# Sigmoid attention and a GELU feed-forward block on one core: a float64 weight decoder that reads raw words two bytes further on

## The chip, the cores and the metric

The program runs on one core of a Trainium2 chip. The metric is the time of one execution in microseconds on the device, as the median of several runs. The engines of the core run side by side, each through its own list of instructions in order: TensorE (PE in the profile; its weight loads are a row of their own, PEld), VectorE (DVE), ScalarE (ACT), GpSimd (POOL, which here only issues transfers) and SyncE (SP, which issues most of the loads). They wait for one another through semaphores.

## The reference

Attention without a softmax, with a sigmoid in its place, and then a two-layer feed-forward block over its output:

```python
batch, n_heads, seq, head_dim = (8, 12, 448, 64)
scores = scale * np.matmul(q, k.transpose(0, 1, 3, 2)) - np.log(S)
attn = 1.0 / (1.0 + np.exp(-scores))
attn_out = np.matmul(attn, v)                      # then [3584 tokens, 768]
h = x @ w_in                                       # 768 x 2048
g = 0.5 * h * (1.0 + erf(h * inv_sqrt2))
return g @ w_out                                   # 2048 x 768
```

`q`, `k` and `v` are fp32. `w_in` and `w_out` come out of the setup as float64, since an fp32 array is multiplied with a float64 scalar. The host only lays the data out anew, so the kernel gets the weights as 64-bit words and makes fp32 of them itself.

## The kernel before

**Attention** is a loop over 24 units of four heads (`u`, 0 to 23; batch `u // 3`). A unit's scores are six tiles of 128 keys by 2 x 448 queries, in the order (p, c) = (0,0), (0,1), (0,2), (1,0), (1,1), (1,2); each is made by six matmuls on q and k split in two fp32r parts (L381). ScalarE turns each tile into a sigmoid (L359). Then `values(u)` multiplies the sigmoids with v (L414) in two passes; between the passes come a tiny VectorE copy called `mark` (L441), for which TensorE waits, and the last 64 keys of the next unit (L398). At the end of a unit, `park` copies the result out of PSUM with two VectorE copies (L453) and sends it to DRAM.

PSUM has four slots of two banks for all this. `place` alternates them, so that the result of unit u (`pav`) lies in the slot that the fourth score tile, (1,0), of unit u + 1 takes. That tile's first weight load therefore waits for both L453 copies.

**The feed-forward block** starts directly after the last unit (L526 for all matmuls). Each weight tile of 128 x 768 is loaded from scratch DRAM (`wst`), copied to fp32r on ScalarE (L255, the high part) and subtracted on VectorE (L262, the low part). The first weight pass (`ffn1_plain`) takes 16 such tiles: steps (0,0), (1,0), (2,0), (3,0) for the first token half, then (0,1), (1,1), (2,1), (3,1), then (4,0) and so on; a step has 18 matmuls. `whl` has four buffers, so tile 4 is prepared only once (0,1) is through. The second token half, `x1`, is loaded when attention ends and split by two casts on ScalarE (L290) and two subtractions on VectorE (L291). Later blocks use sums and differences of quarter weights (a seven-product scheme); for `w_out` these come from `mix`, four VectorE instructions of 512 columns on four decoded quarters, whose results go to DRAM through POOL. `mix` has one output tile `s`, so a second `mix` waits until the transfers of the first are through.

**The weight decoder** runs beside attention and the first weight pass. It is a generator (`Decoder.work`); `dec.go(n)` emits the next n steps where it is called. In a unit that is `decode(u, 0)`, after the scores, and `decode(u, 1)`, inside `meanwhile`, behind `mark`. For a chunk i, `start(i)` makes mantissa and exponent (three VectorE instructions), `scale(i)` runs two ScalarE passes, `end(i)` puts the result together (two VectorE instructions) and issues the raw load of chunk i + 3. `STEPS` says how many steps a unit takes at each place, (1, 2) unless listed; in the feed-forward block `dec.to` spreads the rest over the weight tiles. There are 16 chunks of `w_in` (768 columns) and 24 of `w_out` (512 columns).

The order of all this is written out by hand: the pools run under a manual schedule, and the queues keep the program order.

Of the kernel before, what the change touches and what calls it, by code (L numbers as in the profile page):

```python
# [8 lines left out]
F32 = mybir.dt.float32  # L9
F32R = mybir.dt.float32r  # L10
U32 = mybir.dt.uint32
I32 = mybir.dt.int32
I64 = mybir.dt.int64
# [3 lines left out]
P = 128  # L17
# [4 lines left out]
def tile_sigmoid_attention_gelu_ffn(  # L22
# [27 lines left out]
    def psum(name, bufs):  # L50
# [11 lines left out]
    RAW = 2 * max(WU, 2 * S)  # L62
# [39 lines left out]
    class Decoder:  # L102
# [7 lines left out]
        def load(self, i):  # L110
            if i < len(CHUNKS):
                kind, u, c0, w = CHUNKS[i][:4]
                src = (w_in if kind == "in" else w_out)[u].rearrange("p a b -> p (a b)")
                raw = sb.tile([P, RAW], U32, tag="raw", name=f"raw{i}", bufs=3)[:, : 2 * w]
                nc.sync.dma_start(raw.bitcast(I64), src[:, c0 : c0 + w])
                self.raws[i] = raw.rearrange("p (n t) -> p n t", t=2)

        def start(self, i):
            w = CHUNKS[i][3]
            low, high = self.raws[i][:, :, 0], self.raws[i][:, :, 1]  # L120
            me = sb.tile([P, 2 * WU], U32, tag="me", name=f"me{i}", bufs=2)
            m, e = me[:, :w], me[:, WU : WU + w]
# [7 lines left out]
            self.parts[i] = m, e  # L130

        def scale(self, i):
            e = self.parts[i][1]
# [5 lines left out]
        def end(self, i):  # L139
            kind, u, c0, w, ij, group = CHUNKS[i]  # L140
            high = self.raws.pop(i)[:, :, 1]
            m, e = self.parts.pop(i)
# [768 lines left out]
```

## Time and profile before

| | |
|---|---|
| median of 3 runs | 1024.38 us (1023.8 to 1024.64) |
| the profiled execution | 1023.69 us, span 1021.9 us |
| TensorE busy | 1017.6 us |
| VectorE busy | 726.0 us |
| ScalarE busy | 652.5 us |
| POOL busy | 116.4 us |
| attention, from its first score tile to the feed-forward block's first matmul | 4.27 to 241.79 us |
| TensorE's clock granted | 0.999 of full speed |

The span runs from the first to the last instruction; the time of the execution has 1.8 us more around it. The profile's own times are counted from the start of the span. The profiled execution lies 0.69 us under the median of the runs.

### The profile page before, as it was taken

To read this page: it belongs to the slowest core of one execution; us is meant where nothing else is said; L and a number is where in the kernel's file an instruction comes from. 1 tells how busy PE (TensorE), PEld (TensorE's weight loads), DVE (VectorE), ACT (ScalarE), POOL (GpSimd) and SP (SyncE) were. 2 spreads that over 40 slices of the span, in tenths; PEclk is the share of its full clock that TensorE was granted. 3 is DMA by queue.
4 is the path that set the end of the run, shared out by engine and by line. 5 is a ranking of instruction groups with operands and counts; after the bars stand their busy time and mean duration, and the time that the engine had idled before them with its cause. 6 is when DMAs were issued, how large, how long until landed. Compare 5 with 4: busy or idle time off the path is not lost.

```text
span 1021.9 us, 16631 instructions
## 1 busy us (share of the span) xinstructions
PE 1017.6 (100%) x6478; PEld 921.9 (90%) x6478; DVE 726.0 (71%) x903; ACT 652.5 (64%) x912; POOL 116.4 (11%) x186
## 2 busy tenths in 40 slices
PE   9999999999999999999999999999999999999998
PEld 5656656667999999999999999999999999999998
DVE  3777777885899698795378887434888764368873
ACT  5888887785455466557666655666656467666652
POOL 0111112101332362224000001000000000000000
PEclk9999999999999999999999999999999999999999
DMA  9999899996788797689444445634444553334441
GB/s 265 298 321 322 307 325 303 341 288 226 241 273 278 255 326 274 212 305 337 123 131 126 141 133 166 212 123 126 132 113 147 154 161 113 120 100 133 138 136 67
DMA packets 85998, 211.86 MB, mean 207 GB/s; under 512 B 9440, under 2 KB 35936, under 8 KB 85920
## 3 DMA queue, kind: packets, MB, share of 16 engines
q1 hardware_dynamic: 69136, 153.82, 49.8%
q0 software_dynamic: 14880, 55.26, 15.1%
q10 hardware_dynamic: 1904, 1.72, 0.5%
q8 instruction: 51, 0.84, 0.3%
q14 instruction: 27, 0.22, 0.1%
HBM read 163.38 MB, written 50.33 MB: 209 GB/s over the span
## 4 chain that ended last, share of the span: by engine, by line
PE 99%; DMA 0%; ACT 0%; SPq 0%; issue 0%; ACTq 0%
PE pf L526 76%; PE pav L414 12%; PE sc L381 9%; PE sc_t L398 2%; PE pav L429 0%; PE warm L468 0%; DMA out_dram<-tmp 0%; ACT tmp L784 0%; ACT tmp L779 0%; SPq L728 0%; ACTq L779 0%
## 5 line engine op out<-in xcount | busy, mean ns | idle before, releaser
L526 PE MATMUL pf<-op,whl 128*128 128x448 f32 x2016 | 382.0, 353 | 0.0
L526 PEld LDWEIGHTS pf<-op,whl 128*128 128x128 f32 x2016 | 381.1, 189 | 0.3
L255 ACT CAST whl<-wst 128x768 fp32r<-128x768 f32 x212 | 176.3, 833 | 202.0 <-PE pf L526 185.1
L262 DVE TENSOR_TENSOR whl<-wst,whl 128x768 fp32r<-128x768 f32 x212 | 202.1, 954 | 138.8 <-ACT whl L255 138.5
L526 PE MATMUL pf<-xh_p,whl 128*128 128x448 f32 x1008 | 273.5, 353 | 0.0
L526 PEld LDWEIGHTS pf<-xh_p,whl 128*128 128x128 f32 x1008 | 190.7, 189 | 0.1
L526 PE MATMUL pf<-xl_p,whl 128*128 128x448 f32 x504 | 177.7, 353 | 0.0
L359 ACT ACTIVATE a<-sc 128x896 f32<-128x896 f32 x144 | 119.3, 935 | 32.2 <-PE sc L381 32.2
L414 PE MATMUL pav<-a,v 64*64 64x448 f32 x1296 | 132.8, 541 | 0.0
L563 DVE TENSOR_TENSOR op<-g,op 128x896 fp32r<-128x896 f32 x112 | 121.3, 1083 | 6.6 <-ACT op L573 6.6
L414 PEld LDWEIGHTS pav<-a,v 64*64 64x64 f32 x1296 | 55.1, 132 | 61.3 <-issue 34.6
L573 ACT CAST op<-g 128x896 fp32r<-128x896 f32 x112 | 104.7, 936 | 2.6 <-PE pf L526 2.6
L526 PE MATMUL pf<-xh,whl 128*128 128x448 f32 x384 | 104.3, 353 | 0.0
L526 PEld LDWEIGHTS pf<-xl_p,whl 128*128 128x128 f32 x504 | 95.4, 189 | 0.0
L526 PEld LDWEIGHTS pf<-xh,whl 128*128 128x128 f32 x384 | 72.6, 189 | 0.7 <-issue 0.7
L563 DVE TENSOR_TENSOR g<-g,g 128x896 f32<-128x896 f32 x64 | 69.3, 1083 | 0.0
L526 PE MATMUL pf<-xl,whl 128*128 128x448 f32 x192 | 67.7, 353 | 0.0
L560 ACT ACTIVATE g<-pf 128x448 f32<-128x448 f32 x80 | 41.9, 537 | 20.1 <-PE pf L526 20.1
L134 ACT ACTIVATE me<-me 128x512 f32<-128x512 int32 (+1 forms) x40 | 29.6, 741 | 33.8 <-DVE me L123 33.8
L381 PE MATMUL sc<-lo,hi 64*128 64x448 f32 x276 | 51.2, 367 | 0.0
L351 DVE TENSOR_TENSOR lo<-qk,hi 128x896 fp32r<-128x896 f32 x46 | 50.1, 1089 | 1.1
L381 PE MATMUL sc<-hi,lo 64*128 64x448 f32 x276 | 48.8, 349 | 0.0
(82 smaller groups left out, 875.6 us busy)
## 6 DMA issues: line engine op xcount, KB each, us to landing
wst<-scr_out SPq DMA_DIRECT2D x112, 384.0 KB, 3.1
wst<-scr_in SPq DMA_DIRECT2D x84, 384.0 KB, 3.1
v<-v_dram SPq DMA_DIRECT2D x24, 512.0 KB, 8.0
raw<-w_in_dram SPq DMA_DIRECT2D x16, 768.0 KB, 5.0
raw<-w_out_dram SPq DMA_DIRECT2D x24, 512.0 KB, 5.3
scr_x<-x POOLq DMA_DIRECT2D x24, 448.0 KB, 7.8
qk<-q_dram SPq DMA_DIRECT2D x23, 448.0 KB, 10.1
qk<-k_dram SPq DMA_DIRECT2D x46, 224.0 KB, 10.4
```

What stands on the lines that cost most here:

```text
L134: nc.scalar.activation(e.bitcast(F32), e.bitcast(I32), AF.Relu, bias=1151.0 * 2**23, scale=-8.0)
L255: nc.scalar.copy(hl[:, 0], t)
L262: nc.vector.tensor_tensor(hl[:, 1], t, hl[:, 0], op=ALU.subtract)
L351: nc.vector.tensor_tensor(lo, raw, hi, op=ALU.subtract)
L359: nc.scalar.activation(to, sc, AF.Sigmoid, bias=NEG_LOG_S, scale=SCALE)
L381: nc.tensor.matmul(sc[:, j], ks[rows(j), 1, keys], braid(qs[rows(j), 0]) if braided else qs[rows(j), 0], start=n == 0, stop=n == last,)
L398: nc.tensor.matmul(sc[rows(p), j], raw[rows(j), p, 1, FULL * P :], raw[rows(j), p, 0], start=True, stop=True,)
L414: nc.tensor.matmul(pav[rows(j), p], vals[u][half, p, j, c], a[p][half, j], start=not swap and c == order[0], stop=c == (order[-1], FULL - ...
L526: nc.tensor.matmul(bank, a, braid(m), **flags)
L560: nc.scalar.activation(straight(dst), unbraid(src), AF.Gelu)
L563: nc.vector.tensor_tensor(out, a, b, op=op)
L573: nc.scalar.copy(op[:, 0], src)
```

## The change

Each raw load starts two bytes later in the row. Of every 64-bit word, the first 32-bit word in SBUF then holds bits 16 to 47, and the third 16-bit half holds the top 16 bits (sign, exponent, four bits of mantissa). ScalarE reads that half as a 16-bit integer, strided by 8 bytes, and makes of it the upper part of the fp32 pattern as a 32-bit integer, in two passes. VectorE then needs three instructions for a chunk, all in `end`: shift the word right by 13 and OR it with the upper part, take the rounding bit out of the word (in place), and add the two as integers. `start` is gone, and a chunk has two steps instead of three. The chunks of `w_out` are 1024 columns wide and 12 instead of 24. `STEPS` is new: (1, 1) unless listed, and half the pace in units 18 to 21. The raw tiles grow from 1792 to 2048 words, and the pool of sigmoid tiles shrinks from 11 to 8.

```diff
-    RAW = 2 * max(WU, 2 * S)
+    RAW = 2 * max(WU, 2 * S, 2 * QUAD)
...
-    CHUNKS = [("in", u, 0, WU, 0, 0) for u in range(NF)] + [
-        ("out", 2 * ee + h, c * QUAD, QUAD, ij, (c, e))
+    CHUNKS = [(w_in[u : u + 1].rearrange("r p a b -> p r (a b)"), WU, "in", u, 0, 0) for u in range(NF)]
+    CHUNKS += [
+        (w_out_part(c, e + KE * i), 2 * QUAD, "out", 0, 2 * QUAD * i, (c, e))
         for c in range(2)
         for e in range(KE)
-        for ij, (ee, h) in enumerate(((e, 0), (e, 1), (e + KE, 0), (e + KE, 1)))
+        for i in range(2)
     ]
...
         def load(self, i):
-                raw = sb.tile([P, RAW], U32, tag="raw", name=f"raw{i}", bufs=3)[:, : 2 * w]
-                nc.sync.dma_start(raw.bitcast(I64), src[:, c0 : c0 + w])
+                src = CHUNKS[i][0].bitcast(U16)
+                dst = raw.bitcast(U16)[:, : 4 * w].rearrange("p (r n) -> p r n", r=rows)
+                nc.sync.dma_start(dst[:, :, : 4 * w // rows - 1], src[:, :, 1:])
...
-        def start(self, i):
-            nc.vector.tensor_scalar(e, high, 0x7FF00000, None, op0=ALU.bitwise_and)
-            nc.vector.tensor_scalar(
-                m, high, 11, 0x80000000, op0=ALU.logical_shift_left, op1=ALU.bitwise_or
-            )
-            nc.vector.scalar_tensor_tensor(
-                m, low, 21, m, op0=ALU.logical_shift_right, op1=ALU.bitwise_or
-            )
...
         def scale(self, i):
-            nc.scalar.activation(
-                e.bitcast(F32), e.bitcast(I32), AF.Relu, bias=1151.0 * 2**23, scale=-8.0
-            )
-            nc.scalar.activation(e, e.bitcast(F32), AF.Relu, bias=255.0 * 2**23, scale=-1.0)
+            half = self.raws[i].bitcast(I16)[:, : 4 * w].rearrange("p (n t) -> p n t", t=4)
+            nc.scalar.activation(
+                top.bitcast(F32), half[:, :, 2], AF.Prelu, bias=-LEAST, scale=-1.0, alpha=TINY
+            )
+            nc.scalar.activation(
+                top.bitcast(I32),
+                top.bitcast(F32),
+                AF.Prelu,
+                bias=-LEAST * 2.0**20,
+                scale=-(2.0**19) / TINY,
+                alpha=TINY,
+            )
...
         def end(self, i):
-            nc.vector.scalar_tensor_tensor(
-                e, high, 0x80000000, e, op0=ALU.bitwise_and, op1=ALU.bitwise_or
-            )
-            nc.vector.scalar_tensor_tensor(
-                self.out[:, ij * QUAD : ij * QUAD + w],
-                m,
-                2.0**-31,
-                e.bitcast(F32),
-                op0=ALU.mult,
-                op1=ALU.mult,
-            )
+            nc.vector.scalar_tensor_tensor(
+                bits, words, 13, top, op0=ALU.logical_shift_right, op1=ALU.bitwise_or
+            )
             nc.vector.tensor_scalar(
+                words, words, 12, 1, op0=ALU.logical_shift_right, op1=ALU.bitwise_and
             )
+            nc.vector.tensor_tensor(bits, bits, words, op=ALU.add)
...
-            self.start(0)
-            yield
             for i in range(len(CHUNKS)):
                 self.scale(i)
-                yield
-                if i + 1 < len(CHUNKS):
-                    self.start(i + 1)
                 yield
                 self.end(i)
                 self.load(i + 3)
...
-    STEPS = {2: (1, 1), B * NU - 1: (4, 4)}
+    STEPS = {18: (1, 0), 19: (0, 1), 20: (1, 0), 21: (0, 1)}
...
-            a = at.tile([P, 2, S], F32, tag="a", name=f"a{u}_{p}_{c}", bufs=11)
+            a = at.tile([P, 2, S], F32, tag="a", name=f"a{u}_{p}_{c}", bufs=8)
...
-                dec.go(STEPS.get(u, (1, 2))[place])
+                dec.go(STEPS.get(u, (1, 1))[place])
...
-                dec.to(done + (2 + 3 * len(CHUNKS) - done) * (f + 1) / (NF - 3))
+                dec.to(done + (1 + 2 * len(CHUNKS) - done) * (f + 1) / (NF - 3))
```

The integer add is built as an instruction that the listing calls ISA; it reads each 32-bit word as two 16-bit halves, which is why its row has twice the columns. The new file is three lines shorter ahead of the attention code, so L438 there is the `mark` copy (L441 before), L450 is `park` (L453 before) and L259 is the low part (L262 before).

The first place is VectorE in unit 19, from the copy `mark` to `park`. `raw16` and `me16` belong to chunk 16, the first of `w_out`; `xl0_0` is a part of the first token half's low part, made in this unit because it is one of the last. Before:

```order
L123 TENSOR_SCALAR me17_2491<-raw17_2270 128x512
L124 TENSOR_SCALAR me17_2491<-raw17_2270 128x512
L127 SCALAR_TENSOR_TENSOR me17_2491<-raw17_2270,me17_2491 128x512
L441 COPY ones_63<-pav19_2495 128x2
L143 SCALAR_TENSOR_TENSOR me16_2365<-raw16_2141,me16_2365 128x512
L148 SCALAR_TENSOR_TENSOR wd16_2514<-me16_2365 128x512
L495 TENSOR_TENSOR xl0_0_2171<-xl0_0_2171,xh0_0_2170 128x1344
L453 COPY x19_2541<-pav19_2495 128x448 x2
```

The same place in the changed kernel:

```order
L438 COPY ones_63<-pav19_2456 128x2
L151 SCALAR_TENSOR_TENSOR wd16_2474<-raw16_2000,me16_2339 128x1024
L154 TENSOR_SCALAR raw16_2000<-raw16_2000 128x1024
L157 ISA wd16_2474<-raw16_2000,wd16_2474 128x2048
L492 TENSOR_TENSOR xl0_0_2147<-xl0_0_2147,xh0_0_2146 128x1344
L450 COPY x19_2501<-pav19_2456 128x448 x2
```

The three instructions ahead of `mark` are gone, and between `mark` and the copies out of PSUM there are now three of 1024 columns instead of two of 512. Unit 21 reads alike, with two L259 subtractions where L492 stands here; unit 22 has the three alone.

The second place is VectorE at the start of the feed-forward block, from the first `mix` (output `s0_0`) to the low part of weight tile 4 (`whl4`). Before:

```order
L99 TENSOR_TENSOR s0_0_3108<-wd16_2514,s0_0_3108 128x512
L123 TENSOR_SCALAR me24_3184<-raw24_3007 128x512
L124 TENSOR_SCALAR me24_3184<-raw24_3007 128x512
L127 SCALAR_TENSOR_TENSOR me24_3184<-raw24_3007,me24_3184 128x512
L143 SCALAR_TENSOR_TENSOR me23_3011<-raw23_2974,me23_3011 128x512
L148 SCALAR_TENSOR_TENSOR wd20_2972<-me23_3011 128x512
L96 TENSOR_TENSOR s0_1_3190<-wd20_2972 128x512
L97 TENSOR_TENSOR s0_1_3190<-s0_1_3190,wd20_2972 128x512
L98 TENSOR_TENSOR s0_1_3190<-wd20_2972 128x512
L99 TENSOR_TENSOR s0_1_3190<-wd20_2972,s0_1_3190 128x512
L262 TENSOR_TENSOR whl4_3180<-wst4_2766,whl4_3180 128x768
```

The same place in the changed kernel:

```order
L107 TENSOR_TENSOR s0_0_3034<-wd16_2474,s0_0_3034 128x512
L104 TENSOR_TENSOR s0_1_3046<-wd18_2831 128x512
L105 TENSOR_TENSOR s0_1_3046<-s0_1_3046,wd18_2831 128x512
L106 TENSOR_TENSOR s0_1_3046<-wd18_2831 128x512
L107 TENSOR_TENSOR s0_1_3046<-wd18_2831,s0_1_3046 128x512
L151 SCALAR_TENSOR_TENSOR wd20_3123<-raw20_2711,me20_3120 128x1024
L154 TENSOR_SCALAR raw20_2711<-raw20_2711 128x1024
L157 ISA wd20_3123<-raw20_2711,wd20_3123 128x2048
L259 TENSOR_TENSOR whl4_3118<-wst4_2714,whl4_3118 128x768
```

The second `mix` follows the first at once, and a chunk's three instructions stand behind it and ahead of the low part of tile 4; before, the decoder's work stood between the two `mix` blocks and the low part came right behind the second.

## Rows read from the trace of the kernel before

**Rows 1.** The page's first part: busy us, share of the span, instructions of TensorE and others.
```profile
PE 1017.6 (100%) x6478; PEld 921.9 (90%) x6478; DVE 726.0 (71%) x903; ACT 652.5 (64%) x912; POOL 116.4 (11%) x186
```
**Rows 2.** Stretches of one unit: length, busy us of PE, PEld, DVE, ACT, POOL, clock, DMA.
```profile
16.66:26.61 9.95, 9.95 (x103) 5.93 (x102) 5.08 (x8) 6.71 (x8) 0.84 (x1) 1.00 1.06 323
36.42:46.24 9.82, 9.82 (x103) 6.12 (x102) 7.67 (x11) 8.83 (x11) 1.29 (x2) 1.00 1.07 258
...
85.48:95.29 9.81, 9.81 (x102) 6.09 (x102) 7.67 (x11) 8.27 (x10) 1.28 (x2) 1.00 0.96 309
```
**Rows 3.** The chain that ended last, by time: start us, us, what.
```profile
203.19 3.60 PE sc L381 x36
...
222.81 3.60 PE sc L381 x36
...
241.79 774.28 PE pf L526 x4092
```
**Rows 4.** Timeline of unit 8, ScalarE and VectorE: start us, us, what.
```profile
92.00 0.84 ACT L137 ACTIVATE me<-me 128x768 uint32<-128x768 f32 x1
92.34 0.16 DVE L441 COPY ones<-pav 128x2 f32<-128x2 f32 x1 [1.02 <-PE pav L414]
95.37 1.16 DVE L453 COPY x<-pav 128x448 f32<-128x448 f32 x2 [1.02 <-PE pav L414]
```
**Rows 5.** Timeline of unit 20, TensorE's weight loads: the fourth score tile, the first value.
```profile
204.74 0.19 PEld L381 LDWEIGHTS sc<-lo,hi 64*128 64x128 f32 x2
...
206.72 0.21 PEld L414 LDWEIGHTS pav<-a,v 64*64 64x64 f32 x8 [0.28 <-ACT a L359]
```
**Rows 6.** Groups by line and form: busy us, mean ns of one, idle before.
```profile
L262 DVE TENSOR_TENSOR whl<-wst,whl 128x768 fp32r<-128x768 f32 x212 | 202.1, 954 | 138.8 <-ACT whl L255 138.5
L563 DVE TENSOR_TENSOR op<-g,op 128x896 fp32r<-128x896 f32 x112 | 121.3, 1083 | 6.6 <-ACT op L573 6.6
L573 ACT CAST op<-g 128x896 fp32r<-128x896 f32 x112 | 104.7, 936 | 2.6 <-PE pf L526 2.6
L563 DVE TENSOR_TENSOR xl_p<-x,xh_p 128x1344 fp32r<-128x1344 f32 x12 | 18.7, 1556 | 7.3 <-ACT xh_p L586 7.3
L143 DVE SCALAR_TENSOR_TENSOR me<-raw,me 128x768 uint32<-128x768 uint32 x16 | 15.5, 969 | 0.0
L137 ACT ACTIVATE me<-me 128x768 uint32<-128x768 f32 x16 | 13.5, 843 | 0.5
L123 DVE TENSOR_SCALAR me<-raw 128x768 uint32<-128x768 uint32 x16 | 9.0, 563 | 0.0
```
**Rows 7.** Timeline of VectorE in unit 19.
```profile
200.24 0.16 DVE L441 COPY ones<-pav 128x2 f32<-128x2 f32 x1 [0.87 <-PE pav L414]
...
201.76 1.55 DVE L495 TENSOR_TENSOR xl<-xl,xh 128x1344 fp32r<-128x1344 f32 x1
203.28 1.15 DVE L453 COPY x<-pav 128x448 f32<-128x448 f32 x2
```
**Rows 8.** Timeline of VectorE in unit 21.
```profile
219.86 0.16 DVE L441 COPY ones<-pav 128x2 f32<-128x2 f32 x1 [0.88 <-PE pav L414]
...
223.00 1.15 DVE L453 COPY x<-pav 128x448 f32<-128x448 f32 x2
```
**Rows 9.** Timeline of VectorE at the start of the feed-forward block.
```profile
255.30 1.56 DVE L291 TENSOR_TENSOR xl<-xl,xh 128x1344 fp32r<-128x1344 f32 x1 [2.34 <-ACT xh L290]
...
264.75 0.69 DVE L96 TENSOR_TENSOR s<-wd 128x512 f32<-128x512 f32 x1 [1.79 <-DMA scr_out<-s]
...
266.69 0.68 DVE L99 TENSOR_TENSOR s<-wd,s 128x512 f32<-128x512 f32 x1
267.29 0.95 DVE L262 TENSOR_TENSOR whl<-wst,whl 128x768 fp32r<-128x768 f32 x1
```
**Rows 10.** The load of v issued in unit 3 (L334): duration ns, start us; issue to landing.
```profile
L334 SPq DMA_DIRECT2D v<-v_dram x1: 379/379/379, 44.8 to 44.8; - x1
...
DMA to landing us min/median/max: 9.3/9.3/9.3
```

More of the change, by code (lines that the diff above doesn't have):

```diff
@@ L12 @@
 I32 = mybir.dt.int32
-I64 = mybir.dt.int64
+I16 = mybir.dt.int16
+U16 = mybir.dt.uint16
 AF = mybir.ActivationFunctionType
@@ L85, in tile_sigmoid_attention_gelu_ffn, with w_out_part @@
     }
-    CHUNKS = [("in", u, 0, WU, 0, 0) for u in range(NF)] + [
-        ("out", 2 * ee + h, c * QUAD, QUAD, ij, (c, e))
+    LEAST, TINY = 896.0 * 16, 2.0**-40
+    def w_out_part(c, ee):
+        src = w_out[2 * ee : 2 * ee + 2].rearrange("h p a b -> p h (a b)")
+        return src[:, :, c * QUAD : c * QUAD + QUAD]
+    CHUNKS = [(w_in[u : u + 1].rearrange("r p a b -> p r (a b)"), WU, "in", u, 0, 0) for u in range(NF)]
+    CHUNKS += [
+        (w_out_part(c, e + KE * i), 2 * QUAD, "out", 0, 2 * QUAD * i, (c, e))
         for c in range(2)
         for e in range(KE)
-        for ij, (ee, h) in enumerate(((e, 0), (e, 1), (e + KE, 0), (e + KE, 1)))
+        for i in range(2)
     ]
@@ L111, in load @@
             if i < len(CHUNKS):
-                kind, u, c0, w = CHUNKS[i][:4]
-                src = (w_in if kind == "in" else w_out)[u].rearrange("p a b -> p (a b)")
-                raw = sb.tile([P, RAW], U32, tag="raw", name=f"raw{i}", bufs=3)[:, : 2 * w]
-                nc.sync.dma_start(raw.bitcast(I64), src[:, c0 : c0 + w])
-                self.raws[i] = raw.rearrange("p (n t) -> p n t", t=2)
-        def start(self, i):
-            w = CHUNKS[i][3]
-            low, high = self.raws[i][:, :, 0], self.raws[i][:, :, 1]
-            me = sb.tile([P, 2 * WU], U32, tag="me", name=f"me{i}", bufs=2)
-            m, e = me[:, :w], me[:, WU : WU + w]
-            nc.vector.tensor_scalar(e, high, 0x7FF00000, None, op0=ALU.bitwise_and)
+                src = CHUNKS[i][0].bitcast(U16)
@@ new lines, in load, with scale @@
+                rows, w = src.shape[1], CHUNKS[i][1]
+                raw = sb.tile([P, RAW], U32, tag="raw", name=f"raw{i}", bufs=3)
+                dst = raw.bitcast(U16)[:, : 4 * w].rearrange("p (r n) -> p r n", r=rows)
+                nc.sync.dma_start(dst[:, :, : 4 * w // rows - 1], src[:, :, 1:])
+                self.raws[i] = raw
+        def scale(self, i):
+            w = CHUNKS[i][1]
+            me = sb.tile([P, 2 * WU], U32, tag="me", name=f"me{i}", bufs=2)
+            self.parts[i] = top = me[:, :w]
+            half = self.raws[i].bitcast(I16)[:, : 4 * w].rearrange("p (n t) -> p n t", t=4)
[10 more added lines that the diff above has]
+            )
@@ new lines, in end @@
+        def end(self, i):
+            _, w, kind, u, at, group = CHUNKS[i]
+            words = self.raws.pop(i)[:, : 2 * w].rearrange("p (n t) -> p n t", t=2)[:, :, 0]
+            top = self.parts.pop(i)
+            if at == 0:
+                self.out = sb.tile([P, 4 * QUAD], F32, tag="wd", name=f"wd{i}", bufs=2)
+            bits = self.out[:, at : at + w].bitcast(U32)
+            nc.vector.scalar_tensor_tensor(
+                bits, words, 13, top, op0=ALU.logical_shift_right, op1=ALU.bitwise_or
+            )
@@ L124, in start @@
             nc.vector.tensor_scalar(
-                m, high, 11, 0x80000000, op0=ALU.logical_shift_left, op1=ALU.bitwise_or
+                words, words, 12, 1, op0=ALU.logical_shift_right, op1=ALU.bitwise_and
             )
-            nc.vector.scalar_tensor_tensor(
-                m, low, 21, m, op0=ALU.logical_shift_right, op1=ALU.bitwise_or
-            )
-            self.parts[i] = m, e
-        def scale(self, i):
-            e = self.parts[i][1]
-            nc.scalar.activation(
-                e.bitcast(F32), e.bitcast(I32), AF.Relu, bias=1151.0 * 2**23, scale=-8.0
-            )
-            nc.scalar.activation(e, e.bitcast(F32), AF.Relu, bias=255.0 * 2**23, scale=-1.0)
@@ L139, in end @@
[L139 to L142, printed above, removed]
-            nc.vector.scalar_tensor_tensor(
-                e, high, 0x80000000, e, op0=ALU.bitwise_and, op1=ALU.bitwise_or
-            )
-            if ij == 0:
-                self.out = sb.tile([P, 4 * QUAD], F32, tag="wd", name=f"wd{i}", bufs=2)
-            nc.vector.scalar_tensor_tensor(
-                self.out[:, ij * QUAD : ij * QUAD + w],
-                m,
-                2.0**-31,
-                e.bitcast(F32),
-                op0=ALU.mult,
-                op1=ALU.mult,
-            )
+            nc.vector.tensor_tensor(bits, bits, words, op=ALU.add)
@@ L158, in end @@
                 self.done += 1
-            elif ij == 3:
+            elif at + w == 4 * QUAD:
                 self.pending.append((group, self.out))
```

## The prediction

> **What bounds the kernel now.** I read the busy times first. TensorE is busy for 1017.6 of 1021.9 us [rows 1], so no other engine's saving can be worth more than about 4 us unless that row hides waits. Whether it does is told by the units of attention: unit 1, in which the decoder does nothing yet, lasts 9.95 us with 5.08 us of VectorE work; units 3 and 8 carry a chunk each, 7.67 us of VectorE work, and last 9.82 and 9.81 us [rows 2]. The decoder costs TensorE nothing today. In the feed-forward block 4092 matmuls take 774.28 us [rows 3], 0.189 us apiece without a gap. So there is nothing to win, and the question is only whether the new order makes TensorE wait.
>
> **Where TensorE could wait for VectorE in attention.** The fourth score tile of a unit takes the PSUM slot that both L453 copies of the unit before must empty. In unit 8 the copies start at 95.37 and end 1.16 us later, at 96.53 [rows 4]; the next unit starts at 95.29. In unit 20, which starts at 203.19 [rows 3], the first weight load of the fourth tile stands at 204.74 [rows 5], so it is needed 1.55 us after a unit's start, which is 96.84 for unit 9. The copies have a margin of 0.31 us. What they exceed it by stops TensorE, less some of the 0.28 us that it waits there for a sigmoid anyway [rows 5]; I credit 0.2.
>
> **Prices.** VectorE's two-source instructions take 954, 1083 and 1556 ns at 768, 896 and 1344 columns [rows 6], 1.056 ns a column. The shift with OR has L143's form: 0.97 us at 768 columns, 1.24 at 1024. The rounding bit has L123's: 0.56 us (its 563 ns for 768 columns is far under a column a cycle of the others), and at half the slope 0.70 for 1024; it writes strided, which no row does, so its upper bound is the full rate of L143, 0.97 and 1.24. The integer add has no like in the trace. It reads 1536 or 2048 halves. Its lower bound is L262's rate, a word a step: 0.95 us, and 0.95 + 256 x 1.056 = 1.22 us. Its upper bound is a half a step: 1556 + 192 x 1.056 = 1.76 us, and 1556 + 704 x 1.056 = 2.30 us. The halves of a word lie side by side, and L143 reads just such strided words at the rate of L262, so the lower end is nearer; I take a quarter of the way up, 1.15 and 1.5. With 0.05 us of gaps a chunk costs 2.73 us (768) or 3.49 us (1024) of VectorE.
>
> The Trainium skill, "VectorE: DVE Perf Modes", What auto-detection actually checks, says that an instruction whose tensors are all 16-bit with step one runs two elements a cycle. By it the add would stand at its lower end and the sum below would be about 1.1 us smaller. No row of before has a 16-bit instruction, so the trace neither bears this out nor contradicts it.
>
> **Units 2 to 17: nothing.** Before, `end` came a unit after `scale`; now it follows in the same unit, so the first VectorE instruction waits for the second ScalarE pass. That ended at 92.84 [rows 4], after `mark` at 92.34, which stays ahead. The ScalarE passes are two as before, at the same place of its queue; the first reads strided 16-bit numbers, which I price like L137, 843 ns [rows 6]. Then 92.87 + 2.73 = 95.60, and the copies can start at about 95.52 instead of 95.37: 0.15 of the margin of 0.31 is used. At the upper bounds the chain would be 1.0 us longer and each unit would lose about 0.6 us, 16 times: some 9 us. The removed instructions ahead of `mark` stood in VectorE's idle time (1.02 us before `mark` [rows 4]), so they give nothing back.
>
> SP's queue moves too: the raw load waits for its buffer until the add is through, about 2 us later, and the loads of v, q and k stand behind it. It also comes one unit earlier at the start (unit 2 instead of 3), where the DMA engines are full (1.07 [rows 2]). The tightest is v of unit 5: issued at 44.8, landed 9.3 us later, at 54.1 [rows 10]. Unit 5 starts two units after 36.42, at 56.04, and its values come 3.5 us later (206.72 against 203.19 [rows 3, 5]), at 59.6. With 2.4 us of later issue and a raw load more in front (0.79 MB at some 300 GB/s [rows 2], 2.6 us) it lands at 59.1. I put nothing in the sum, and up to 2 us in the range. The eight sigmoid buffers cost nothing: seven are used in a unit, and TensorE ends a unit's values before it begins the next scores.
>
> **Unit 19: 1.4 us.** VectorE goes from `mark` at 200.24 to the copies at 203.28 with two 512-column instructions and the 1.55 us of L495 [rows 7]. Now: 200.32 + 3.49 = 203.81, L495 until 205.28, the copies from 205.2 to 206.36 (successive instructions overlap by 0.08). They are needed at 203.19 + 1.55 = 204.74. Late by 1.62; less 0.2 is 1.4 us.
>
> **Unit 21: 1.65 us.** `mark` at 219.86 [rows 8]; 219.94 + 3.49 = 223.43; two low parts, 1.82 us, until 225.17; the copies until 226.25, needed at 222.81 + 1.55 = 224.36. Late by 1.89, less 0.2.
>
> **Unit 22: 0.5 us.** Scale and end fall together with 1024 columns. In unit 8 the second pass ended 7.36 us after the unit's start; at ScalarE's slope ((936 - 843) / 128 = 0.73 ns a column [rows 6]) each pass is 0.19 us longer, so it ends at 7.74, and VectorE at 7.74 + 3.49 = 11.23, the copies at 12.3. Needed: 9.81 + 1.55 = 11.36. That is 0.95 late, less 0.2, less what unit 22 has already been held up in its middle by unit 21's copies, which stops TensorE more than ScalarE. I take 0.5, between 0 and 0.8. Units 18 and 20 only scale, and a pass longer by 0.19 us meets the wait for the next unit's scores.
>
> **Start of the feed-forward block: 2.6 us.** Step (4,0) comes after 8 steps of 18 matmuls, 144 x 0.189 = 27.25 us after 241.79 [rows 3]: at 269.04 it needs the low part of tile 4, which was ready at 267.29 + 0.95 = 268.24 [rows 9], a margin of 0.8 us. The second `mix` can't start before the transfers of the first have left `s` (264.75, released by DMA), and ends at 267.37 [rows 9]. Before, the decoder's work stood in that wait; now both `mix` blocks follow one another, the wait is empty, and a chunk of 3.49 us stands between the second `mix` and the low part: 267.29 + 3.49 = 270.78, the low part from 270.7 to 271.65. Late by 2.6 us. Afterwards VectorE catches up: a chunk less than every 6.8 us, so later tiles are ready in time. The split of `x1` is close too: its last low part ends at 256.86 [rows 9] and is needed half a step into (0,1), at 241.79 + 13.6 + 1.7 = 257.1. The raw load of 1 MB that now falls beside its transfers may cost up to 1 us; I put 0 in the sum.
>
> **The sum.** 1.4 + 1.65 + 0.5 + 2.6 = 6.15 us on the profiled execution's 1023.69, of which the span is 1021.9: 1029.8 us. The median of the runs lies 0.69 above it, so 1030.5 us. With the add at its lower end the four terms are 5.1 us together. With add and rounding bit at their upper ends each of the four chains is 1.3 us longer, and the ordinary units lose as well: 6.15 + 5.2 + 9 = 20 us, 1044.7.
>
> **The rivals.** *Hidden after all: 1024.4 to 1026.4 us.* A margin that I don't see takes the delays, such as first `mix` transfers that land earlier because no raw load runs beside them, by 2.6 us; then 268.1 is reached and two or three us are left of the sum, or less. Against it: the rows give the two late copies without a transfer in them. *Faster: about 1018 us.* If TensorE's busy row hid waits for ScalarE, 0.28 us in each of 23 units is 6 us, and less VectorE work could free some of it. It decides only if a unit without decoding is shorter, and unit 1 is not [rows 2]. *The ordinary units stall as well: 1034 to 1045 us*, if the add takes a half a step or the strided write halves the rounding bit's rate; the margin of 0.31 us decides, and 0.2 us more per unit is 3 us. *The shifted load is slow: 1045 us and more.* Raw loads are 0.79 of some 3 MB a unit (9.81 us at 309 GB/s); if each took twice the DMA time, a unit's share would go from 0.96 to 1.2 [rows 2] and 16 units would grow by about 2 us each, 30 us. Only the rows of the start address differ; nothing in the trace speaks for twice the time.
>
> **How the numbers follow.** The forecast, four places that wait and no others, gets 0.66 and lies between 1027 and 1034. The hidden case gets 0.14, the ordinary units 0.12, the slow load 0.05, faster 0.03. What a measurement of this kernel can tell from no change is about 0.2%, 2 us: faster 0.03, same 0.13 (nearly all of the hidden case), slower 0.84. The range of 1025 to 1039 takes in the forecast, most of the hidden case and half of the ordinary units' one, and leaves out less than 2 in 10.
>
> **What would show it.** Right: TensorE's weight loads of the fourth score tile in units 20, 22 and 23 wait for L450, 1.4, 1.7 and some 0.5 us; units 2 to 17 last 9.81 us; a weight load about 27 us after the feed-forward block's start waits some 2.6 us for L259; VectorE's busy time falls. Wrong: an add of over 1.3 us at 768 columns, a rounding bit of over 0.7, raw loads that land later by more than the shift of their issue, or no wait at tile 4.

## The result, and the profile after

The changed kernel takes 1035.7 us (median of 4 runs, 1030.79 to 1038.87) against 1024.28 us before (4 runs, 1023.8 to 1024.64): ratio 1.0108, 95% interval [1.0093, 1.0122]. It is slower, and it is also less steady: the kernel before stays within 0.9 us, the changed one spreads over 8. Among the executions of the kernel before that stand beside the experiments a few took longer, up to 1029.07 us, so it is not wholly free of such cases. One execution of experiment 8 (2007.59 us) and one of the kernel before beside experiment 12 (1126.37 us) ran at a mean granted clock of 0.82 and 0.89 and are left out of the ratios below. The profiled execution is the fastest of the four, 1030.79 us with a span of 1029.0, 7.1 us more than the profiled one before. What follows therefore explains 7 us from this trace and needs other traces for the rest.

TensorE's waits in the changed kernel (what it waited for: us in total, times, longest). Before, this view had only the last row, under that kernel's line numbers:

```profile
PE sc L378 <- DVE x L450: 2.5, 2, 1.4
PE pav L411 <- DMA v<-v_dram: 1.7, 1, 1.7
PE pf L523 <- DVE whl L259: 1.4, 1, 1.4
PE warm L465 <- PEq L898: 0.8, 1, 0.8
```

Stretches of one unit each, units 8, 18 to 22 (length, busy us of PE, PEld, DVE, ACT, POOL, clock, DMA share, GB/s), which answer to [rows 2]:

```profile
85.36:95.17 9.81, 9.81 (x104) 6.08 (x100) 6.34 (x10) 8.35 (x10) 1.27 (x2) 1.00 1.00 312
183.43:193.24 9.81, 9.81 (x105) 6.08 (x101) 4.78 (x8) 8.90 (x10) 1.30 (x2) 1.00 1.04 360
193.24:204.76 11.52, 9.84 (x104) 6.08 (x100) 7.26 (x10) 7.25 (x9) 0.71 (x1) 1.00 1.04 339
204.76:215.94 11.18, 10.05 (x104) 5.62 (x101) 7.88 (x10) 9.31 (x11) 0.71 (x1) 1.00 1.05 332
215.94:225.75 9.81, 9.81 (x105) 6.08 (x102) 7.22 (x10) 7.35 (x10) 0.71 (x1) 1.00 0.68 191
225.75:237.17 11.42, 10.04 (x104) 5.61 (x100) 9.06 (x13) 8.31 (x10) 0.71 (x1) 1.00 0.74 248
```

An ordinary unit still lasts 9.81 us, with a VectorE that has less to do (6.34 against 7.67 us). Unit 19 is 1.71 us longer, unit 20 1.37, unit 22 1.61. Units 20 and 22 are the two predicted waits for `park`, with the predicted sizes; that of unit 19 is not in the prediction's sum: it is for v. VectorE in unit 19, the place of [rows 7], with the chunk's three instructions ahead of L492 and `park`:

```profile
201.89 0.16 DVE L438 COPY ones<-pav 128x2 f32<-128x2 f32 x1 [3.97 <-PE pav L411]
201.97 1.22 DVE L151 SCALAR_TENSOR_TENSOR wd<-raw,me 128x1024 uint32<-128x1024 uint32 x1
203.22 0.70 DVE L154 TENSOR_SCALAR raw<-raw 128x1024 uint32<-128x1024 uint32 x1
203.96 1.23 DVE L157 CUSTOM_DVE_ANT_0 wd<-raw,wd 128x2048 uint16<-128x2048 uint16 x1
205.10 1.55 DVE L492 TENSOR_TENSOR xl<-xl,xh 128x1344 fp32r<-128x1344 f32 x1
206.57 1.15 DVE L450 COPY x<-pav 128x448 f32<-128x448 f32 x2
```

The copies end at 207.72, and TensorE's weight loads (idle time in brackets) of the fourth score tile start right behind, in unit 20 and in unit 22; the third row is unit 23, the fourth is the weight load that needs the low part of tile 4 in the feed-forward block:

```profile
207.84 0.21 PEld L378 LDWEIGHTS sc<-lo,hi 64*128 64x128 f32 x2 [1.45 <-issue]
229.07 0.21 PEld L378 LDWEIGHTS sc<-lo,hi 64*128 64x128 f32 x2 [1.70 <-issue]
239.05 0.21 PEld L378 LDWEIGHTS sc<-lo,hi 64*128 64x128 f32 x2 [0.26 <-issue]
275.46 0.19 PEld L523 LDWEIGHTS pf<-xh,whl 128*128 128x128 f32 x1 [1.75 <-DVE whl L259]
```

What stands behind v's lateness is SP's queue. The load of v for unit 19 in the changed kernel (duration ns, start us; issue to landing), and behind it the same load before:

```profile
L331 SPq DMA_DIRECT2D v<-v_dram x1: 419/419/419, 184.3 to 184.3; - x1
...
DMA to landing us min/median/max: 14.2/14.2/14.2
```

```profile
L334 SPq DMA_DIRECT2D v<-v_dram x1: 392/392/392, 182.1 to 182.1; - x1
...
DMA to landing us min/median/max: 11.9/11.9/11.9
```

It is issued 2.15 us later (184.26 against 182.11), since the raw load ahead of it in the queue waits until the add has read the buffer, and takes 2.3 us longer, beside a raw load of twice the size. It lands at 198.46; the values would have started 1.7 us earlier. The five places add up to 6.6 us (1.71 + 1.37 + 1.61 + 0.2 + 1.75); after the last matmul the transfers of the result took 6.4 us instead of 5.8, which covers the rest of the 7.1.

The prices, by line and form (busy us, mean ns, idle before):

```profile
L157 DVE CUSTOM_DVE_ANT_0 wd<-raw,wd 128x1536 uint16<-128x1536 uint16 x16 | 15.3, 958 | 0.6
L157 DVE CUSTOM_DVE_ANT_0 wd<-raw,wd 128x2048 uint16<-128x2048 uint16 x12 | 14.7, 1225 | 0.4
L151 DVE SCALAR_TENSOR_TENSOR wd<-raw,me 128x1024 uint32<-128x1024 uint32 x12 | 14.7, 1221 | 14.9 <-ACT me L135 13.6 <-DMA scr_out<-s 1.2
L154 DVE TENSOR_SCALAR raw<-raw 128x768 uint32<-128x768 uint32 x16 | 9.1, 566 | 0.6
```

### The profile page after: what moved, and what is told of

It reads as the page before. It is cut to its first block, busy times and chain, and to the rows that moved or that the text cites. A ratio compares the mean times of both kernels' runs of the same rounds, so it can differ in the third digit from the quotient of the medians.

```text
span 1029.0 us, 16508 instructions
## 1 busy us (share of the span) xinstructions
PE 1018.5 (99%) x6478; PEld 920.3 (89%) x6478; DVE 675.1 (66%) x787; ACT 652.3 (63%) x888; POOL 116.3 (11%) x186
## 3 DMA queue, kind: packets, MB, share of 16 engines
q0 software_dynamic: 14880, 55.26, 14.7%
## 4 chain that ended last, share of the span: by engine, by line
PE 94%; DMA 2%; issue 1%; DVE 1%; POOL 0%; ACTq 0%; ACT 0%; SPq 0%; DVEq 0%; POOLq 0%
PE pf L523 73%; PE pav L411 11%; PE sc L378 8%; PE sc_t L395 2%; DMA v<-v_dram 1%; PE pav L426 0%; DMA scr_out<-wd 0%; DMA xl<-scr_x 0%; PE warm L465 0%; POOL scr_out L173 0%; DVE wd L151 0%; DVE whl L259 0%; DVE x L450 0%; DVE raw L154 0%; DMA out_dram<-tmp 0%
## 5 line engine op out<-in xcount | busy, mean ns | idle before, releaser
L259 DVE TENSOR_TENSOR whl<-wst,whl 128x768 fp32r<-128x768 f32 x212 | 202.0, 954 | 150.4 <-ACT whl L252 150.1
L438 DVE COPY ones<-pav 128x2 f32<-128x2 f32 x23 | 3.7, 159 | 73.3 <-PE pav L411 73.3
L378 PE MATMUL sc<-hi 64*128 64x448 f32 x276 | 49.0, 349 | 0.0
## 6 DMA issues: line engine op xcount, KB each, us to landing
qk<-k_dram SPq DMA_DIRECT2D x46, 224.0 KB, 11.2
```

Of the source, the lines that this page charges most:

```text
L259: nc.vector.tensor_tensor(hl[:, 1], t, hl[:, 0], op=ALU.subtract)
L378: nc.tensor.matmul(sc[:, j], ks[rows(j), 1, keys], braid(qs[rows(j), 0]) if braided else qs[rows(j), 0], start=n == 0, stop=n == last,)
L438: nc.vector.tensor_copy(mark, pav[:, :, 0])
```

## The experiments

Every kernel was run against the kernel before on the same chip (median before 1024.04 to 1024.33). Ratios are to the kernel before, with 95% intervals; the changed kernel itself stands at 1.011.

**1. The changed kernel again.** 

> The changed kernel unchanged. Theory (four places where VectorE's chain is late, and on top of them loads of v that land late in units 18 and 19, by another amount in each execution): TensorE again waits for the park copies in units 20 and 22, 1.1 to 1.4 us each, and 1.4 us for the low part of tile 4; the wait for v differs from the 1.7 us of the first profile, anywhere from 0 to 8 us; the times spread over at least 3 us, median 1030 to 1038. Rival (the spread is the chip's and has nothing to do with the kernel): the kernel before spreads as much in the same call.

1034.69 us (6 runs, 1032.46 to 1038.82), 1.0109 [1.0091, 1.0128], while 11 runs of the kernel before lay between 1023.58 and 1024.66. The two waits for `park` are the same 2.5 us to the digit; the matmul that needs the low part of tile 4 waits 2.4 us instead of 1.4, and v delays units 18 and 19 (10.41 and 10.83 us long). The slower executions also have a lower mean granted clock, 0.997 and 0.998 against 1.000 in the profiled one. So two of the four places are fixed in size and two are not.

**2. The width undone, the decoder kept.** w_out in 24 chunks of 512, one a unit:

```diff
-        src = w_out[2 * ee : 2 * ee + 2].rearrange("h p a b -> p h (a b)")
+        src = w_out[ee : ee + 1].rearrange("h p a b -> p h (a b)")
...
-    STEPS = {18: (1, 0), 19: (0, 1), 20: (1, 0), 21: (0, 1)}
+    STEPS = {B * NU - 1: (4, 2)}
```

> Undoes the width alone: w_out in 24 chunks of 512 columns, one per unit again, the new decoder otherwise kept. Theory (the width makes both the long VectorE chains and the 1 MB loads that delay v): no wait of TensorE over 0.3 us in units 18 to 23, tile 4 waits under 0.6 us, 1023.5 to 1026 us with a spread under 1.5 us. Rival (the two-byte shift makes raw loads dear, whatever the width): the 16 loads of w_in are as before, v still lands late, 1029 us or more.

1029.09 us (1028.69 to 1031.09), 1.0053 [1.004, 1.0066]. Neither side is right alone. The `park` waits are gone from this view, as the theory said (units 20 to 22 together are still 0.4 us longer), and half of the loss is gone; but 5.0 of 10.6 us stay, and TensorE's waits name them:

```profile
PE pf L523 <- DVE xl L288: 1.1, 1, 1.1
PE pf L523 <- DVE whl L259: 1.1, 1, 1.1
PE pav L411 <- DMA v<-v_dram: 0.8, 1, 0.8
...
PE pf L523 <- ACT xh L287: 0.7, 1, 0.7
```

v, x1 and tile 4 are late with 512 columns too. So the width makes 5.6 us here (1034.69 - 1029.09); the other 5.0 stay with the new decoder and its pace at 512 columns. That pace has a part of its own that was not separated: unit 23 takes (4, 2) steps, its raw loads at 242.86 and 244.64 stand beside x1, and the second cast of x1 starts 14.9 us after the block.

**3. The end step behind `park` from unit 18 on**, and so its raw load behind v.

```diff
                     split_qk(1, 0)
                     split_qk(1, 1)
-                decode(u, 1)
+                if u < 18:
+                    decode(u, 1)
...
             load_v(u + 2)
+            if u >= 18:
+                decode(u, 1)
```

> From unit 18 on the decoder's end step stands behind the park copies and behind the load of v, instead of ahead of both. Theory: the waits of units 20 and 22 for the park copies go (2.5 to 3.2 us with what they pass on), tile 4's wait stays at 1.4 us; the loads of chunks 16 to 18 that stand ahead of v stay, so the spread stays; fastest executions about 1028 us. Rival (the chain's late end is hidden by another wait right behind it, such as the sigmoid's): less than 1 us is won.

1033.72 us (6 runs, 1030.62 to 1041.22), 1.0108 [1.0082, 1.0134]: by the time alone, inconclusive. In the trace the waits for `park` are gone and units 20 and 22 last 10.31 us instead of 11.18 and 11.42. Of the 3.0 us, 1.0 comes back at once: the splits of the next q and k now stand behind the chunk, `mark` is late, and a value's weight load waits 0.99 us for it instead of 0.3. The rest drowns in the spread of v and tile 4 (2.3 us in this profile).

**4. Every raw load behind v.**

```diff
...
                 self.end(i)
-                self.load(i + 3)
+                self.later = i + 3
...
             load_v(u + 2)
+            dec.late_load()
```

> Every raw load during attention is issued behind the load of v of the same unit instead of ahead of it; VectorE's order is as in the changed kernel. Theory: no wait for v; what is left is the VectorE waits, 1028.5 to 1030.5 us with a spread under 2 us. Rival (the DMA engines are full at that time, and the order of the issues doesn't matter): v lands as late, 1030 to 1039 us as before. Second rival (the raw loads now land too late themselves): ScalarE's first pass waits for a raw load, over 1031 us.

1033.94 us (1030.14 to 1035.47), 1.0092 [1.0078, 1.0107]. v is never waited for, and in units 9 to 17 it lands 8 to 11 us ahead instead of 2.7 to 4.1. But unit 3 lost 1.4 us to k, at the start where all loads are late, and tile 4 was waited for longest so far, 2.9 us. What follows that wait shows where lower mean clocks like those of experiment 1 can come from (stretches; the column before the DMA share is the granted clock):

```profile
276.00:278.00 2.00, 0.00 (x0) 0.00 (x0) 2.00 (x2) 1.97 (x3) 2.00 (x4) 1.00 0.47 133
278.00:280.00 2.00, 1.86 (x8) 1.79 (x9) 2.00 (x4) 0.64 (x1) 1.29 (x2) 0.82 1.04 221
280.00:282.00 2.00, 2.00 (x7) 1.81 (x6) 1.93 (x3) 0.00 (x0) 0.00 (x0) 0.50 0.96 280
282.00:284.00 2.00, 2.00 (x10) 1.92 (x10) 1.93 (x3) 0.47 (x1) 0.00 (x0) 0.83 0.98 363
```

TensorE did nothing for 2.9 us, and then the clock stood at its lower level, 1.2 GHz, for 3.4 of the next six microseconds: 2 x (0.18 + 0.50 + 0.17) = 1.7 us lost beyond the wait itself. This one stretch makes the mean clock of the execution 0.998.

**5. The decoder one weight tile later in the feed-forward block.** Chunk 20 no longer stands between the second `mix` and the low part of tile 4:

```diff
-                dec.to(done + (1 + 2 * len(CHUNKS) - done) * (f + 1) / (NF - 3))
+                dec.to(done + (1 + 2 * len(CHUNKS) - done) * f / (NF - 4))
```

> The decoder's share of the feed-forward block begins one weight tile later, so that the low part of tile 4 stands right behind the second mix again, without a chunk of 3.1 us between; attention is unchanged. Theory (the low part of tile 4 is late by a chain that begins with the landing of x1 and was 17.6 us long in the changed kernel, 14.3 us before): the chain is 14.5 us again, TensorE's wait there (1.4, 2.4 and 2.9 us in three profiles) goes to 0 in the fast executions, those without a wait keep the clock at 1.00, and the spread narrows: 1028.5 to 1034 us, median about 3.5 us under the changed kernel. Rival (the wait only moves to the next tile, as VectorE has the chunk to do anyway): tile 5's low part is waited for instead and less than 1 us is won.

1031.53 us (6 runs, 1030.76 to 1034.45), 1.0077 [1.0065, 1.009], about 3 us less than the changed kernel. The wait for tile 4 is gone, and no other tile took its place. In this execution v was late in unit 19 and, by 0.1 to 0.3 us, in units 8, 9 and 11 as well, where the profile after shows a margin; unit 3 lost 0.4 us to k.

**6 and 9. The raw load of unit 23 away from x1.** In the first attempt only the place in the program moved, behind x1's split:

```diff
...
                     dec.pool = late
                     dec.flush()
+                    dec.hold = False
+                    dec.late_load()
```

> The raw load issued in unit 23 (1 MB, at the moment when the second token half's x1 is loaded) is held back until both halves of x1 are split. Theory (x1 and this load share the DMA engines): the second half of x1 lands 2 to 3 us earlier after the block's start, TensorE's waits for x1 go and that for tile 4 shrinks by as much; median 2 to 4 us under the changed kernel. Rival (x1 waits for the writing of the last unit's result, not for bandwidth): it lands as late, no change.

1034.49 us (4 runs, 1033.73 to 1034.74), 1.0098 [1.0085, 1.0112]. This told nothing about x1: SP has nothing to wait for there, and issued the load at 248.78, as in the changed kernel (248.46). It gave one thing by chance. TensorE waited 3 us for tile 4 here too, and the clock did not fall:

```profile
276.00:280.00 4.00, 1.02 (x6) 0.68 (x5) 3.93 (x5) 3.38 (x4) 3.09 (x5) 1.00 0.66 179
280.00:282.00 2.00, 2.00 (x13) 2.00 (x12) 2.00 (x3) 0.00 (x0) 0.59 (x1) 1.00 0.97 225
```

So a wait of this length sometimes costs the clock and sometimes not. The second attempt puts the load on ScalarE's queue, behind the second cast:

```diff
...
                 if f == 1:
+                    dec.hold = False
+                    for i in dec.held:
+                        dec.load(i, nc.scalar)
                     dec.pool = late
```

> The raw load of unit 23 is now issued on ScalarE's queue, behind the second cast of x1, so that it can't run beside x1's transfers (in the run before, SP issued it at the same moment as in the changed kernel, so nothing had been held). Theory (this 1 MB load slows x1): the second half of x1 lands within 9 us of its issue instead of 9.5 to 12.9, no wait for x1's low part, tile 4's wait under 2 us; median 2 us or more under the changed kernel. Rival (the writes that POOL issues at that time, or the transfer of x1 itself, set it): it lands as late and the median is that of the changed kernel.

1031.0 us (6 runs, 1029.96 to 1032.06), 1.0063 [1.0047, 1.0078], some 4 us less than the changed kernel (3.6 by the medians, each against the kernel before beside it). The second cast of x1 starts 8.1 us after the block, not 11.2, and neither x1 nor tile 4 is waited for:

```profile
PE sc L382 <- DVE x L454: 2.5, 2, 1.4
PE pav L415 <- DMA v<-v_dram: 2.5, 1, 2.5
```

Here v came late by 2.5 us in unit 19, and the clock fell behind that wait as in experiment 4, with 1.7 us lost:

```profile
200.00:202.00 2.00, 2.00 (x16) 0.91 (x12) 0.00 (x0) 0.00 (x0) 0.00 (x0) 0.54 1.05 307
202.00:204.00 2.00, 2.00 (x16) 0.82 (x12) 0.00 (x0) 0.00 (x0) 0.00 (x0) 0.61 1.03 400
```

The profile of experiment 10 has a third such stretch, behind a wait of 2.0 us for tile 4 (granted 0.95, 0.50 and 0.70 from 276 to 282 us). After waits of 2.3 and 2.4 us for tile 4, in experiments 3 and 1, the clock stayed at 1.00, so the length of the wait alone does not tell which it will be.

**7. Four repairs together, width 1024.** Those of experiments 3, 5 and 6, and raw loads behind v from unit 14 on.

> The width of 1024 kept, with four repairs: the end step behind park and v from unit 18 on, raw loads behind v from unit 14 on, the raw load of unit 23 behind x1, and the decoder's share of the feed-forward block one tile later. Theory (these are all the places): no wait of TensorE over 0.5 us, clock 1.00, 1024 to 1026 us with a spread under 1.5 us. Rival (a wait that these only uncover, or a slowdown by the two-byte shift itself): 1028 us or more.

1026.91 us (5 runs, 1026.5 to 1028.51), 1.0033 [1.002, 1.0046]. Most of it is back, but not all: x1's low part is waited for 0.8 us (its load was not really held, see above), and units 20 and 22 last 10.31 us, the late `mark` of experiment 3.

**8. Width 512 with the same repairs except that of `park`.**

> The new decoder with w_out 512 wide, and the three repairs that don't concern the width (raw loads behind v from unit 14 on, the last of them behind x1, the decoder one tile later in the feed-forward block). Theory: level with the kernel before, 1023 to 1025 us; it can't be much faster, since TensorE was busy all the time before. Rival (the new decoder costs something that none of these touch): 1026 us or more.

1024.54 us (median of 11 runs, of which ten lie between 1024.15 and 1025.05), 1.0002 [0.9993, 1.0011]: level with the kernel before. TensorE waits 0.5 us for v in unit 0, and in this view for nothing else of the change; units 20 to 22 together are still 0.5 us longer. With its loads in this order the new decoder costs nothing that the interval shows; it also wins nothing, since TensorE was never short of VectorE.

**10. Raw loads from the start of the row.** The length is the same, and so are the instructions behind the loads, which now take other bits for the weight: the result is of no use, and only the time is read.

```diff
-                nc.sync.dma_start(dst[:, :, : 4 * w // rows - 1], src[:, :, 1:])
+                nc.sync.dma_start(dst[:, :, : 4 * w // rows - 1], src[:, :, : 4 * w // rows - 1])
```

> The raw loads start at the beginning of the row, not two bytes on, with the same length and the same instructions behind them, which then decode the wrong bits. Theory (the start address costs nothing; v is late because the raw load and v stand in SP's queue behind the integer add, 2 us later in a unit, among other transfers): as the changed kernel, 1030 to 1039 us, the w_in loads land in 6.4 us, v's margin in units 6 to 17 is 2 to 4 us. Rival (the shifted start slows the load): the w_in loads land in 5 us as before the change, v's margin is over 5 us, 2 us or more are won.

1035.87 us (6 runs, 1032.41 to 1039.61), 1.0112 [1.0089, 1.0135]: as with the shift. v of units 6 to 16 still takes 8.2 to 10.1 us to land (with the shift 8.5 to 9.9, before 6.1 to 8.4), and its margin is 2.5 to 4.4 us. A raw load of w_in lands in 5.5 us (median of the 13 that are issued one by one) instead of 6.3, where it took 4.9 before. But the landing differs as much between executions with the shift: 6.8 us in experiment 1, the same kernel, and 6.2 and 5.9 in experiments 3 and 9, which do not touch these loads. Each load is 128 packets, one row each, and the mean packet of the 13 loads takes 372 ns here, against 374 in the profile after and 366 to 368 in those of experiments 1, 2, 3, 5, 7 and 9. So the start two bytes on costs nothing that these traces show. Before, the packet of 6144 bytes took 308 ns; whether the row of 6142 bytes or the later moment in the unit makes the difference, no run separates.

The Trainium skill's page "DMA: Bandwidth & Descriptors", section "How a descriptor splits into AXI transactions", says that a descriptor that doesn't start on a 256-byte boundary begins with a transaction at the boundary below, and that the bytes ahead of the start still cost beats. An estimate by that rule: if the row itself starts on such a boundary, its 6142 bytes touch the same 24 blocks of 256 bytes from byte 2 as from byte 0, and the shift should cost nothing. The packets agree, 374 against 372 ns.

**11. v one unit earlier, and tile 4 repaired.**

```diff
-            vr = at.tile([P, 2, 2, FULL + 1, D], F32, tag="v", name=f"v{u}", bufs=3)
+            vr = at.tile([P, 2, 2, FULL + 1, D], F32, tag="v", name=f"v{u}", bufs=4)
...
-            load_v(u + 2)
...
+            load_v(u + 3)
...
```

> v has four buffers and is loaded one unit earlier, and tile 4's low part stands right behind the second mix as in the run of that change alone. Theory (late v, by another amount in each execution, made the spread that was left there, 1030.8 to 1034.5): no wait for v, 1027.5 to 1030 us with a spread under 1.5 us; what is left is the two waits for park (3.2 us with what they pass on) and x1. Rival (the loads as a whole are too slow in some executions, so that q and k come late instead): the spread stays over 3 us.

1029.37 us (6 runs, 1028.18 to 1031.43), 1.0049 [1.0033, 1.0065]. No unit waits for v; units 20 and 22 are 11.18 and 11.43 us long as always, and x1 costs 1.5 us (it landed later here, cast 14.65 us after the block's start). The spread is 3.3 us, where 1.5 was expected and the rival had over 3; x1 alone may make that, but no run shows it, and VectorE waits 1.1 us for k in this profile.

**12. Width 1024 with another set of repairs.** Chunks end in units 18, 22 and 23 only; v one unit earlier; the raw load behind x1 as in experiment 9; tile 4 as in 5.

```diff
...
-    STEPS = {18: (1, 0), 19: (0, 1), 20: (1, 0), 21: (0, 1)}
+    STEPS = {19: (0, 0), 20: (0, 0), 21: (0, 0)}
...
```

> The width of 1024 kept, with four repairs: a chunk in units 18, 22 and 23 and none in 19 to 21 (so that no end step meets other VectorE work ahead of park), v one unit earlier, the raw load of unit 23 behind x1's second cast, and the decoder's share of the feed-forward block one tile later. Theory (park, v, x1 and tile 4 are all the places): no wait of TensorE over 0.5 us, clock 1.00, 1024 to 1025.3 us, spread under 1.5 us: level with the kernel before. Rival (something else of the change costs time everywhere): 1026 us or more.

1027.4 us (8 runs, 1026.4 to 1031.05), 1.003 [1.002, 1.0041]. The theory fails in attention. From its start the feed-forward block is as long as before (1029.3 - 248.86 = 780.4 us against 1021.9 - 241.72 = 780.2), so that half is understood. In attention units 3, 19, 21 and 23 are 0.9 to 2.1 us longer in this profile (the slowest of the eight executions). One row of TensorE's waits and one of VectorE's:

```profile
PE sc L382 <- DVE x L454: 1.3, 2, 0.7
...
DVE hi L343 <- DMA qk<-k_dram: 11.5, 5, 4.3
```

Units 19 and 23 wait for `park` again, 0.9 us each. Scale and end of a chunk now fall together in units 18 and 22, VectorE waits 0.9 us for ScalarE's second pass behind `mark`, and the weight load of the fourth score tile in the next unit sits idle for 1.0 us. That is the prediction's chain for unit 22, worked out there as 0.95 us late, with nothing ahead of it that hides it. In units 3 and 21 it is k that is late although v is in time, as the rival of experiment 11 had it. The DMA engines are full there (share 1.03 to 1.05 between 180 and 220 us, before as after), so it seems that with raw loads of 1 MB the order in SP's queue only decides which load pays; that is argued, not shown. At 512 columns experiment 8 has an order in which TensorE waits 0.5 us for one load, and for no other.

## Why the prediction was right, and where it was not

**Nothing to win, four places to lose.** There was nothing to win, and all four places wait. But they are not all: late loads and the clock add to them. 1030.5 was meant and 1035.7 came, outside the 1027 to 1034 that the prediction gave to four places and no others, and inside the 1034 to 1045 of a rival whose mechanism did not come, since units 3 to 17 still last 9.81 us. That the wide range of 1025 to 1039 holds the result is partly luck. The profiled execution's 1030.79 is close to the 1029.8 worked out for it partly by luck too, since 1.7 of its 7.1 us are not in the sum and two terms are smaller than forecast.

**Units 19 and 21.** 1.4 and 1.65 us were forecast (1.89 less 0.2 is 1.69; the slip is small), 1.37 and 1.61 came, and within 0.03 us the same in every trace that keeps this order. The margin worked out from the first weight load of the fourth tile is the step that carried it.

**Unit 22.** 0.5 forecast, 0.2 measured (unit 23's 0.26 us of idle weight load). The stall in the middle of unit 22, by which TensorE is held and ScalarE is not, probably took more than I credited: without such a stall, experiment 12's chunks in units 18 and 22 cost 0.9 us each.

**The add.** 958 and 1225 ns against 1150 and 1500 assumed: the lower end. The step from 1536 to 2048 halves costs 267 ns, half a nanosecond each, as L151 costs 1.03 a word. The Trainium skill's page "VectorE: DVE Perf Modes", section "What auto-detection actually checks", has two elements a cycle for 16-bit tensors of step one, and the row agrees; a page against which nothing in the trace spoke deserved more than a quarter of the way. Since `park` moved by 0.29 us less than forecast but TensorE's weight load starts 0.12 us behind the copies, which I had left out, the error hardly shows.

**Tile 4.** 2.6 forecast; by the weight load's idle time 1.75 here, 2.7 and 3.3 in the profiles of experiments 1 and 4. The chunk does stand in the chain: from the second cast of x1 to the end of the low part [rows 9] it was 14.29 us before, is 17.65 after, and 14.25 in experiment 5. The second cast, before and after:

```profile
253.95 1.31 ACT L290 CAST xh<-xl 128x1344 fp32r<-128x1344 f32 x1 [2.14 <-DMA xl<-scr_x]
```

```profile
257.75 1.31 ACT L287 CAST xh<-xl 128x1344 fp32r<-128x1344 f32 x1 [4.86 <-DMA xl<-scr_x]
```

The block starts at 241.72 before and at 246.55 after, so the cast starts 12.23 and 11.20 us into it. What the prediction held fixed is this beginning of the chain. The first weight load of tile 4 is due 27.16 us after the block's start, so the wait is (cast's start) + 17.65 - 27.16: with the 12.23 of before it would be 2.72, close to the forecast; 11.20 gives 1.69, and 12.59 with experiment 1's chain of 17.30 gives 2.73, both as measured.

**The raw load beside x1: a step that failed.** The prediction said that it may cost up to 1 us and put 0 in the sum. In the profile after, x1's second cast is not late at all, as the 11.20 us show; in the other profiles with a raw load of 1 MB in this place it starts 11.8 to 14.7 us into the block. Taking the load away brought it to 8.1 us and gave some 4 us (experiment 9). The kernel before has raw loads of 512 columns beside x1 itself, so these 4 us are what the place is worth without a load, not what the change added there. What the step left out is that x1's delay passes on to everything chained behind it, tile 4 above all, and that a wait there can cost 1.7 us more through the clock.

**v: the other step that failed.** The later issue was seen, 2.4 us forecast and 2.15 measured, but its margin was taken at unit 5 as the tightest, 5.5 us, and there it holds (4.6 after). In the kernel before it is thinner elsewhere: 1.6 us in unit 3, 1.9 in unit 22, and 2.9 in unit 19, where v lands at 194.0 (182.11 + 11.9) and the first value is loaded at 196.91:

```profile
196.91 0.21 PEld L414 LDWEIGHTS pav<-a,v 64*64 64x64 f32 x8 [0.28 <-ACT a L359]
```

In unit 19 the margin is now below nothing, beside three raw loads of 1 MB issued 10 us apart (164.17, 173.98, 183.79); with 512 columns v was late there too, by 0.8 us (experiment 2). Nothing in the sum and up to 2 us in the range was one execution's size; it differs between executions. As far as the runs show, the spread comes from v, x1 and the clock: 8 us in the changed kernel, 3.3 with v early and tile 4 repaired (experiment 11), 2.1 without the load beside x1 (experiment 9), 0.9 in the ten executions of experiment 8.

**The rivals.** Hidden after all: no. Faster: no. The ordinary units: not through VectorE, whose new chain fits their margin (the strided rounding bit took 566 ns, the row that it was priced by 563); only through v, in some executions. The slow shifted load: no; the shift shows no price (experiment 10), and a packet grew from 308 to 374 ns, not to twice its time. The smaller pool of sigmoid tiles was not run by itself; in the profile after ScalarE waits for no such tile.

**What stays open.** The clock's part in the 1038.87 us execution is known only from its mean, 0.997: 0.3% of its span of 1037.1 us would be about 3 us, an estimate. And the 3 us that are left with 1024 columns are placed at `mark` and x1 (experiment 7) and at `park` and k (experiment 12), but no version without them was found.

## What to carry to other kernels

When an instruction that frees a buffer moves later, follow the queue that refills the buffer: every load behind it in that queue moves too, and each one's margin has to be read, not that of one early place: here it held in unit 5 and failed in unit 19. Take a margin that ends in a DMA as an interval; here a forecast from one trace came near the fastest execution, and the median, with loads that are just in time, lay 5 us above it. Making an engine faster that nobody waits for won nothing, and making its pieces larger lost wherever a short instruction for which another engine waits stood behind them.

## What the runs showed of the hardware

The integer add on 16-bit halves runs at the rate of a 32-bit instruction on half as many words (1225 ns for 2048 halves, 1221 for 1024 words). Waits of TensorE of 2.0, 2.5 and 2.9 us were each followed by 3.4 us at 1.2 GHz (experiments 10, 9 and 4; granted 0.82, 0.50, 0.83 in the last), and waits of 2.3, 2.4 and 3.0 us by full clock (experiments 3, 1 and 6); each fall lost 1.7 us. A two-byte shift of the source left the mean packet of a 768 KB load at 374 ns, against 372 without it, and had no effect on the time that the runs show.
